# Pairing the first two gate/up tiles by weight instead of by tile, with other warm-up matmuls, a free PSUM unit and other places for the score-value runs

## The chip, the cores and the metric

The kernel runs on one core of one Trainium2 chip. The metric is device time in microseconds. The kernel before took 555.25 us (median of three runs, 555.22 to 555.34). One further execution was profiled: 555.64 us, of which 554.4 us lie between its first and last instruction (the span).

## The reference

The input x has 2048 rows of 576 values. It is normalised row by row, and the result xn goes two ways: through attention with a sliding window of 256 keys, 32 heads of 18 values, and through a gated feed-forward of width 4608. The feed-forward's output gates the attention's. All arrays are bf16.

```python
xn = layernorm(x)
qkv = xn @ wqkv                       # 576 -> 3 * 576
p = softmax(mask(q @ k.T * 18**-0.5)) # 256 keys back, causal
s = (p @ v) @ wo
h = sigmoid(xn @ w_gate) * (xn @ w_up)   # 576 -> 4608, twice
g = silu(h @ w_down)                     # 4608 -> 576
out = x + s * g
```

## The kernel before

The rows are worked in four chunks of 512 (NC, NT). For each chunk the program makes a graph of operations: normalisation (build_ln), value projection (build_v), query/key projections (build_qk), scores and exponentials for eight groups of four heads (build_attn), the score-value products (build_pv), the output projection (build_wo), gate/up and down projections (build_ffn) and the closing element-wise work (build_final). A list scheduler in the kernel's own Python (schedule, L1165) then puts all operations in an order for each engine. It has a cost for every operation and for every hand-over from one engine to another, among them 235 ns for a TensorE step that waits for an earlier TensorE step (TURN_WAIT_NS, L84). Each engine works through its list in order; semaphores carry the dependencies. Loads of weights and inputs are issued by the SP queue, also in its listed order.

TensorE works with its array split into two halves of 64 rows. A pair (L119) is two matmuls, one on each half, that run side by side into two PSUM banks; the contraction of 576 is cut into nine pieces of 64, four blocks of 128 rows (two pieces each) and a remainder of 64. A gate/up tile is 128 of the 4608 columns of w_gate and the same of w_up, for the 512 rows of a chunk. Its step "lo" (half 0) runs four pairs in which one half of the array adds the upper pieces of gate and the other half the lower pieces of up; its step "hi" (half 1) runs the same four pairs with the halves exchanged, and a fifth pair for the remainder. "hi" waits for "lo", since both add into the same two banks.

PSUM is used in four units of two banks. Pool S (units 0 and 1) serves scores, projections and transposes, pool F (units 2, 3, 1) gate/up and down, pool V (all four) the score-value runs (L366 to L368). A unit is taken when the scheduler places an operation, and is free again when the operations that read it are done.

The start is special. Gate and up weights for two tiles come as one load each (load_nat, weights at L960; tiles 0 and 1 share a slot). The 512 rows of the first chunk come in four blocks of 128 that are normalised one by one and transposed on TensorE (L644, recorded as L650); ScalarE and VectorE copy the transposes to xnT (L631). Tiles 0 and 1 (NEARLY = 2) don't wait for all blocks: each is cut into three parts (PARTS, L76), block 0, block 1, and blocks 2 and 3 together, and each part has a lo and a hi step of four pairs without the remainder (early_turn, L128; gate_up, L991). The remainder of the rows is transposed last (build_two, L616) and a single pair per tile adds it (last_rows, L1012). The third tile's lo step is placed ahead of tile 1's last hi step (the name ahead). tail (L1023) is ScalarE's tanh and VectorE's product, after which the tile's unit is free.

Before the first transposes, and again between those of block 0 and block 1, TensorE multiplies a zero tile (warm, L496, sizes in WARM, L72): nine pairs of 512 columns and seven of 128, then five pairs of 256.

The score-value products of four head groups are one run of 256 (first chunk) or 384 TensorE instructions, small matmuls of 19 columns (recorded as L854); there are eight runs. RUN_AT (L43) holds for each the position in TensorE's instruction stream before which it is not placed (L1202).

Of the kernel before, what the change touches and what calls it, by code (L numbers as in the profile page):

```python
# [12 lines left out]
P = 128  # L13
# [5 lines left out]
NT = 512  # L19
NC = S // NT  # L20
BPC = NT // P
FG = 4
NFG = NFT // FG
WG = 2
# [15 lines left out]
OENG = ("SP", "POOL")  # L40
PV_ORDER = (0, -4, 1, 7, 2, -3, 3, 6, 4, -2, -1, 5)
TURN_NS = 265.0
RUN_AT = (2093, 3885, 5836, 7411, 9682, 11471, 13542, 15053)  # L43
BINS = (((-4, 0, 1), (1, 1, 5), (6, 6, 2)),
        ((-2, 0, 3), (3, 3, 5)),
        ((0, 0, 5), (5, 5, 3)),
# [48 lines left out]
def mm_ns(n):  # L95
    return max(24.7, n / 2.4 + 2.7)
# [19 lines left out]
BLOCKS = ((1, 2, 3, 4), (1, 2, 3, 4, 0))  # L116


def pair(eng, outs, lhs, rhs, start, stop, swap=0, parts=False):  # L119
    res = None  # L120
    for i in range(2):
        t = i ^ swap
        res = eng.matmul(outs[i], lhs(ROWS[t], i), rhs(ROWS[t], i), start=start, stop=stop, tile_position=(64 * t, 0),  # L123
                         skip_group_check=parts)
    return res


def early_turn(eng, outs, lhs, rhs, hi, first):  # L128
    res = None
    for k in BLOCKS[0]:  # L130
        res = pair(eng, outs, lambda r, t: lhs(r, t, k), lambda r, t: rhs(r, t, k), first and not hi and k == BLOCKS[0][0], False, hi, True)
    return res
# [13 lines left out]

class Hold:

    __slots__ = ("pool", "n", "units", "rel")

    def __init__(self, pool, n):
        self.pool = pool
        self.n = n
        self.units = None
        self.rel = []

    def release(self, op):
        self.rel.append(op)
# [2 lines left out]
class Pool:  # L161
# [27 lines left out]

    def take(self, hold, units):  # L190
        deps = []
        for u in units:
            if self.last[u] is not None:
                deps += self.last[u].rel
            self.last[u] = hold
        hold.units = units
        return deps


class Op:  # L200
    __slots__ = ("eng", "est", "deps", "fn", "name", "prio", "start", "end", "tok", "needs_tok",
                 "nbytes", "slack", "idx", "succs", "cidx", "odeps", "acq", "lane", "filler", "space", "ni", "run", "then")
# [60 lines left out]
class Builder:  # L263
# [231 lines left out]

    def warm(self, groups, dep, before):  # L496
        h, zero = self.warm_h, self.warm_src
        for n, est, count in groups:
            def f_warm(eng, n=n):
                return pair(eng, self.halves(h, n), lambda r, t: zero[r, :],  # L500
                            lambda r, t: zero[r, :][:, None, :].broadcast_to([64, n // P, P]), True, True)
            for i in range(count):
                w = self.op("PE", est, f_warm, f"warm:{n}:{i}", deps=[dep], prio=4, acq=None if before else h, odeps=[before], ni=4)
                w.filler = h
                h.release(w)
                before = w
# [435 lines left out]
    def build_ffn(self, c):  # L942
        op = self.op
        xs = c % 2
        x_in = self.xnT[:, xs, :, :]
        slots = {}
# [40 lines left out]
        def bank(h, w):  # L987
            o = h.units[0] * 1024 + 512 * w
            return self.ps[:, o:o + 512]

        def gate_up(ft, h, half, acq, part=None, deps=(), behind=()):  # L991
            sw, fc = slots[ft // WG], slice((ft % WG) * P, (ft % WG + 1) * P)
            b0, b1 = (0, BPC) if part is None else PARTS[ft][part]
            t0, n = b0 * P, (b1 - b0) * P
            xin = (self.op_xnT[c] if part is None else self.op_x0)[b0:b1]

            def lhs(r, t, k):
                return self.wgs[r, sw, k - 1, t, fc] if k else self.wgr[r, rslots[ft // (2 * WG)], ft % (2 * WG) * P:(ft % (2 * WG) + 1) * P]

            def f(eng):  # L1000
                outs = [bank(h, w)[:, t0:t0 + n] for w in range(2)]
                if part is None:
                    return turn(eng, outs, lhs, lambda r, t, k: x_in[r, k, t0:t0 + n], half)
                return early_turn(eng, outs, lhs, lambda r, t, k: x_in[r, k, t0:t0 + n], half, part == 0)
            steps = len(BLOCKS[half] if part is None else BLOCKS[0])
            o = op("PE", steps * mm_ns(n), f, f"f1{half}:{c}:{ft}", deps=[xin, wops[ft // WG][0:1 + half if part is None else 1], deps],
                   prio=3 if part is None else 1, odeps=chain[half] if part is None else list(behind), acq=acq, ni=4 * steps)
            chain[half] = [o] if part is None else chain[half] + [o]
            self.ffn_last = o
            return o  # L1010

        def last_rows(ft, h, behind):  # L1012
            fc = slice(ft % (2 * WG) * P, (ft % (2 * WG) + 1) * P)

            def f(eng):
                return pair(eng, [bank(h, w) for w in range(2)], lambda r, t: self.wgr[r, rslots[0], fc], lambda r, t: x_in[r, 0, :],
                            False, True, 1, True)
            o = op("PE", mm_ns(NT), f, f"f12:{c}:{ft}", deps=[self.op_xnT[c], wops[0][1]], prio=1, odeps=behind, ni=4)
            chain[1] = chain[1] + [o]
            self.ffn_last = o  # L1020
            return o

        def tail(ft, h, pg):  # L1023
            st, dt_ = self.r_t.produce()
            th = op("ACT", act_ns(NT), lambda e: e.activation(self.tring[:, st, :], bank(h, 0), ACTF.Tanh, scale=0.5),  # L1025
                    f"th:{c}:{ft}", deps=[pg, dt_], prio=0)
            war = [self.prev_f2_last[ft // FG]] if self.prev_f2_last else []
            mu = op("DVE", dve_ns(NT), lambda e: e.scalar_tensor_tensor(  # L1028
                self.hT[:, ft, :], self.tring[:, st, :], 1.0, bank(h, 1), ALU.add, ALU.mult),
                f"hm:{c}:{ft}", deps=[th, pg, war], prio=0)  # L1030
            h.release(mu)
            self.r_t.release(st, mu)
            hm[ft] = mu
# [3 lines left out]
        if early:  # L1037
            weights(0)
            weights(1)
            hs = [self.pool_f.hold() for _ in range(NEARLY)]  # L1040
            for ft, h in enumerate(hs):
                u = None
                for part in range(len(PARTS[ft])):
                    lo = gate_up(ft, h, 0, None if part else h, part, [u])
                    if ft == early - 1 and part == len(PARTS[ft]) - 1:
                        ahead = self.pool_f.hold()
                        ahead = (ahead, gate_up(early, ahead, 0, ahead))
                        chain[1] = chain[1] + [ahead[1]]
                    u = gate_up(ft, h, 1, None, part, [lo], [ahead[1]] if ahead else [])
                u = last_rows(ft, h, [u] + ([ahead[1]] if ahead else []))  # L1050
                tail(ft, h, u)
                if ft == 1:
                    self.r_w.release(slots[0], u)
        for ft in range(early, NFT):
            if ft % WG == 0 and ft // WG not in slots:
                weights(ft // WG)
            if ahead and ft == early:
                h, lo = ahead
            else:
                h = self.pool_f.hold()  # L1060
                lo = gate_up(ft, h, 0, h)
            u = gate_up(ft, h, 1, None, None, [lo])
# [319 lines left out]
```

## Time and profile before

| | |
|---|---|
| median of three runs | 555.25 us |
| profiled execution | 555.64 us |
| its span | 554.4 us |
| TensorE matmuls | 550.1 us busy, 8234 instructions |
| VectorE | 324.3 us |
| ScalarE | 272.3 us |
| GpSimd | 209.1 us |
| HBM read, written | 63.18 MB, 2.36 MB |

A line of the timeline gives the start in us, the time to the last end of a group in us, engine, source line, operation, output and inputs, the shape and the count; in brackets the idle time of that engine before it and what ended it. A matmul's record is longer than its share of the array, because matmuls overlap; the spacing of starts tells the rate. "PE L123" stands for all pairs, since one helper makes them; what a pair belongs to is read from the tile names (wgs: gate/up weights, wgr: their remainder, wqg: query/key weights, wd_sb: down weights, hT as input of a 512-column matmul: warm-up). The chain of waits is the work that ended last, followed back.

### The profile page before, as it was taken

To read this page: it belongs to the slowest core of one execution; us is meant where nothing else is said; L and a number is where in the kernel's file an instruction comes from. 1 tells how busy PE (TensorE), PEld (TensorE's weight loads), DVE (VectorE), ACT (ScalarE), POOL (GpSimd) and SP (SyncE) were. 2 spreads that over 40 slices of the span, in tenths; PEclk is the share of its full clock that TensorE was granted. 3 is DMA by queue.
4 is the path that set the end of the run, shared out by engine and by line. 5 is a ranking of instruction groups with operands and counts; after the bars stand their busy time and mean duration, and the time that the engine had idled before them with its cause. 6 is when DMAs were issued, how large, how long until landed. Compare 5 with 4: busy or idle time off the path is not lost.

```text
span 554.4 us, 19202 instructions
## 1 busy us (share of the span) xinstructions
PE 550.1 (99%) x8234; PEld 337.2 (61%) x8234; DVE 324.3 (58%) x782; ACT 272.3 (49%) x380; POOL 209.1 (38%) x360
## 2 busy tenths in 40 slices
PE   8999999999999999999999999999999999999998
PEld 5465555767545554577755555557776565445887
DVE  5467564854597654746485655764375564865412
ACT  4246562444265764445355565464446663567202
POOL 5734343564346123085423333164536113270020
DMA  8899999242456657353125765273102656350002
GB/s 231 235 259 246 255 261 271 78 84 53 100 152 173 201 164 201 102 131 69 29 58 162 233 186 154 82 198 86 33 20 66 202 169 178 107 146 3 6 21 67
DMA packets 141212, 75.85 MB, mean 137 GB/s; under 512 B 43676, under 2 KB 139260, under 8 KB 141128
## 3 DMA queue, kind: packets, MB, share of 16 engines
q1 hardware_dynamic: 133704, 68.71, 47.1%
q0 software_dynamic: 7424, 5.92, 4.0%
q8 instruction: 65, 1.06, 0.8%
q14 instruction: 19, 0.16, 0.1%
HBM read 63.18 MB, written 2.36 MB: 118 GB/s over the span
## 4 chain that ended last, share of the span: by engine, by line
PE 98%; DMA 1%; SPq 0%; issue 0%; DVE 0%; ACT 0%
PE ps L123 95%; PE ps L854 3%; DMA wgs<-in_B_w_up_dram 1%; SPq L294 0%; PE ps L650 0%; ACT thf L1139 0%; DVE thf L1141 0%; DVE xf L1144 0%
## 5 line engine op out<-in xcount | busy, mean ns | idle before, releaser
L123 PE MATMUL ps<-xnT,wgs 64*128 64x512 bf16 (+2 forms) x2368 | 283.3, 370 | 0.5 <-DMA wgs<-in_B_w_up_dram 0.5
L804 ACT ACTIVATE expr<-ps 128x1024 bf16<-128x1024 f32 (+4 forms) x160 | 155.0, 969 | 99.3 <-PE ps L123 97.8
L123 PEld LDWEIGHTS ps<-xnT,wgs 64*128 64x128 bf16 x2368 | 114.3, 94 | 110.4 <-ACT xnT L631 0.6
L123 PE MATMUL ps<-wd_sb,hT 64*128 64x288 bf16 (+2 forms) x2448 | 153.8, 276 | 0.0
L1028 DVE SCALAR_TENSOR_TENSOR hT<-tring,ps 128x512 bf16<-128x512 bf16 x144 | 98.7, 685 | 82.9 <-ACT tring L1025 80.5
L1025 ACT ACTIVATE tring<-ps 128x512 bf16<-128x512 f32 x144 | 86.2, 598 | 118.5 <-PE ps L123 115.8
L294 POOL DMA_DIRECT2D qk<-qd x160 | 82.9, 524 | 154.4 <-PE ps L123 150.1
L123 PEld LDWEIGHTS ps<-wd_sb,hT 64*128 64x128 bf16 x2448 | 112.7, 94 | 29.9 <-issue 0.6
L817 DVE TENSOR_TENSOR expr<-expr,mask 128x128 bf16<-128x128 bf16 (+2 forms) x240 | 64.2, 294 | 66.9 <-ACT expr L804 64.5
L294 POOL DMA_DIRECT2D oT<-o2T x72 | 36.6, 516 | 125.6 <-DVE ot L885 70.4
L768 POOL TENSOR_SCALAR kx<-kprev,small 128x256 bf16<-128x256 bf16 x64 | 60.8, 960 | 8.0 <-PE ps L123 7.1
L123 PE MATMUL ps<-qk,kx 64*128 64x320 bf16 (+1 forms) x704 | 59.2, 254 | 0.0
L123 PE MATMUL ps<-xnT,wgr 64*128 64x512 bf16 x288 | 55.0, 376 | 0.0
L123 PEld LDWEIGHTS ps<-qk,kx 64*128 64x128 bf16 x704 | 31.8, 94 | 24.9 <-issue 0.4
L123 PE MATMUL ps<-xnT,wqg 64*128 64x512 bf16 (+1 forms) x320 | 37.8, 355 | 0.0
L689 DVE CAST qd<-ps 128x1024 bf16<-128x1024 f32 (+1 forms) x20 | 22.3, 1116 | 8.9 <-PE ps L123 8.8
L882 DVE STREAM_TRANSPOSE ot<-ps 128x512 f32<-128x512 f32 x32 | 20.2, 685 | 11.8 <-PE ps L854 11.8
L768 DVE TENSOR_SCALAR kx<-qk,small 128x512 bf16<-128x512 bf16 x64 | 21.5, 365 | 7.1 <-PE ps L123 6.3
L123 PEld LDWEIGHTS ps<-xnT,wgr 64*128 64x128 bf16 x288 | 14.4, 94 | 16.6
L890 DVE STREAM_TRANSPOSE o2T<-o 128x512 bf16<-128x512 bf16 x32 | 22.6, 706 | 2.5 <-DMA oT<-o2T 2.2
L123 PEld LDWEIGHTS ps<-xnT,wqg 64*128 64x128 bf16 x320 | 15.3, 94 | 11.4
L936 ACT ACTIVATE s_attn<-ps 128x576 bf16<-128x576 f32 x16 | 10.3, 651 | 22.9 <-PE ps L123 22.9
(71 smaller groups left out, 284.4 us busy)
## 6 DMA issues: line engine op xcount, KB each, us to landing
wgs<-in_B_w_gate_dram SPq DMA_DIRECT2D x72, 256.0 KB, 4.1
wgs<-in_B_w_up_dram SPq DMA_DIRECT2D x72, 256.0 KB, 4.3
wd_sb<-in_B_w_down_dram SPq DMA_DIRECT2D x9, 576.0 KB, 6.5
wqg<-in_A_wqkv_dram SPq DMA_DIRECT2D x32, 128.0 KB, 3.9
qk<-qd POOLq DMA_DIRECT2D x100, 36.0 KB, 2.6
wgr<-in_B_w_gate_dram SPq DMA_DIRECT2D x36, 64.0 KB, 2.9
wgr<-in_B_w_up_dram SPq DMA_DIRECT2D x36, 64.0 KB, 3.2
wvo<-in_A_wqkv_dram SPq DMA_DIRECT2D x4, 576.0 KB, 5.5
```

The costliest lines, as they stand in the source:

```text
L123: res = eng.matmul(outs[i], lhs(ROWS[t], i), rhs(ROWS[t], i), start=start, stop=stop, tile_position=(64 * t, 0), skip_group_check=parts)
L294: o = self.op(eng, DMA_ISSUE_NS[eng], lambda e: e.dma_start(dst, src), name, deps, prio, nbytes=nbytes)
L689: return eng.tensor_copy(dst, self.both(h, n))
L768: return e.tensor_scalar(self.kx[:, sx, pos:pos + n_ // SW, t, :], src.rearrange("p (s k) -> p s k", k=SW), self.half[:, t:t + 1], None, A ...
L804: return eng.activation(self.expr[:, se, :, lo * SW:NT], self.both(h, NT)[:, :, lo * SW:NT], ACTF.Exp, scale=SM_SCALE)
L817: return eng.tensor_tensor(e_, e_, m_, ALU.mult)
L854: res = eng.matmul(outs[i][p0:p0 + VH, cols], self.v_aug[ROWS[i], o:o + VH], self.expr[ROWS[i], se, t, cols], start=m == 0, stop=m == len( ...
L882: return e.transpose(self.ot1[:, p1, :], self.halves(hp, NT, un)[i])
L890: t2 = op("DVE", dve_ns(NT), lambda e, p2=p2, p3=p3: e.transpose(self.o2T[:, p3, :], self.o2[:, p2, :]), f"ot2:{c}:{pr}:{i}", deps=[on, d3 ...
L936: return eng.activation(dst, self.both(h2, 288), ACTF.Copy, scale=1.0 if c == NC - 1 else 0.25)
L1025: th = op("ACT", act_ns(NT), lambda e: e.activation(self.tring[:, st, :], bank(h, 0), ACTF.Tanh, scale=0.5), f"th:{c}:{ft}", deps=[pg, dt_ ...
L1028: mu = op("DVE", dve_ns(NT), lambda e: e.scalar_tensor_tensor(self.hT[:, ft, :], self.tring[:, st, :], 1.0, bank(h, 1), ALU.add, ALU.mult) ...
```

## The change

The first two gate/up tiles are worked together. A pair now holds the same weight of both tiles: gate of tile 0 beside gate of tile 1, then up beside up, for one block of rows at a time (four parts in place of three). So a step needs the load of one weight only, and one block. There are 4 parts x 2 weights x 2 halves = 16 steps of four pairs, where there were 2 tiles x 3 parts x 2 halves = 12, four of them of 256 columns. The pool hands out both units at once (first, Hold.each). The third tile's lo step is placed behind all of them, and the remainder pairs of the two tiles, which keep the old pairing of gate with up, wait for the hi step of the other weight.

The fourth tile takes its PSUM unit from pool V, so that it may have unit 0. Of the warm-ups, the wide ones in front become ten single matmuls over all 128 rows, the narrow ones three pairs, and those behind the first transposes two pairs of 512 columns. RUN_AT has eight new values.

```diff
-RUN_AT = (2093, 3885, 5836, 7411, 9682, 11471, 13542, 15053)
+RUN_AT = (2096, 3832, 5614, 7366, 9427, 10958, 13261, 14786)
-WARM = (((512, 427, 9), (128, 107, 7)), ((256, 160, 5),))
+WARM = (((512, 427, 10, 1), (128, 107, 3, 2)), ((512, 320, 2, 2),))
-PARTS = (((0, 1), (1, 2), (2, 4)),) * NEARLY
+PARTS = ((0, 1), (1, 2), (2, 3), (3, 4))
...
     def take(self, hold, units):
         deps = []
-        for u in units:
+        for j, u in enumerate(units):
             if self.last[u] is not None:
                 deps += self.last[u].rel
             self.last[u] = hold
+            if hold.each:
+                self.last[u] = hold.each[j]
+                hold.each[j].units = [u]
...
-        for n, est, count in groups:
+        for n, est, count, tiles in groups:
+                if tiles == 2:
+                    return pair(...)
+                return eng.matmul(outs[0], zero, zero[:, None, :].broadcast_to([P, n // P, P]), start=True, stop=True)
...
+        def early_pairs(part, w, half, deps, acq=None):
+            b0, b1 = PARTS[part]
+            cols = slice(b0 * P, b1 * P)
+
+            def f(eng):
+                res = None
+                for k in BLOCKS[0]:
+                    res = pair(eng, [bank(h, w)[:, cols] for h in hs], lambda r, t: self.wgs[r, slots[0], k - 1, w, t * P:t * P + P],
+                               lambda r, t: x_in[r, k, cols], part == 0 and not half and k == BLOCKS[0][0], False, half, True)
+                return res
+            o = op("PE", len(BLOCKS[0]) * mm_ns((b1 - b0) * P), f, f"f1{half}:{c}:{'gu'[w]}{part}",
+                   deps=[self.op_x0[b0:b1], wops[0][0][w], deps], prio=1, acq=acq, ni=4 * len(BLOCKS[0]))
...
-        def last_rows(ft, h, behind):
+        def last_rows(ft, h, deps, behind):
-            o = op("PE", mm_ns(NT), f, f"f12:{c}:{ft}", deps=[self.op_xnT[c], wops[0][1]], prio=1, odeps=behind, ni=4)
+            o = op("PE", mm_ns(NT), f, f"f12:{c}:{ft}", deps=[self.op_xnT[c], wops[0][1], deps], prio=1, odeps=behind, ni=4)
...
             hs = [self.pool_f.hold() for _ in range(NEARLY)]
-            for ft, h in enumerate(hs):
-                ...
+            first = self.pool_f.hold(NEARLY)
+            first.each = hs
+            hi = [None, None]
+            for part in range(len(PARTS)):
+                ws = (0, 1) if part < len(PARTS) - 1 else (1, 0)
+                lo = [None, None]
+                for w in ws:
+                    lo[w] = early_pairs(part, w, 0, hi[w], first if part == 0 and w == 0 else None)
+                for w in ws:
+                    hi[w] = early_pairs(part, w, 1, lo[w])
+            ahead = self.pool_f.hold()
+            ahead = (ahead, gate_up(early, ahead, 0, ahead))
+            chain[1] = chain[1] + [ahead[1]]
+            tail(0, hs[0], last_rows(0, hs[0], [hi[1]], [hi[0]]))
+            u = last_rows(1, hs[1], [hi[0]], [hi[1], ahead[1]])
+            tail(1, hs[1], u)
...
-                h = self.pool_f.hold()
+                h = (self.pool_v if ahead and ft == early + 1 else self.pool_f).hold()
```

More of the change, by code (lines that the diff above doesn't have):

```diff
@@ L125, in pair @@
     return res
[L128 to L132, printed above, removed]
 def turn(eng, outs, lhs, rhs, hi):
@@ L147 @@
 class Hold:
-    __slots__ = ("pool", "n", "units", "rel")
+    __slots__ = ("pool", "n", "units", "rel", "each")
     def __init__(self, pool, n):
@@ L155, in __init__ @@
         self.rel = []
+        self.each = None
     def release(self, op):
@@ L497, in warm, with f_warm @@
         h, zero = self.warm_h, self.warm_src
-        for n, est, count in groups:
-            def f_warm(eng, n=n):
-                return pair(eng, self.halves(h, n), lambda r, t: zero[r, :],
-                            lambda r, t: zero[r, :][:, None, :].broadcast_to([64, n // P, P]), True, True)
+        for n, est, count, tiles in groups:
+            def f_warm(eng, n=n, tiles=tiles):
+                outs = self.halves(h, n)
+                if tiles == 2:
+                    return pair(eng, outs, lambda r, t: zero[r, :],
+                                lambda r, t: zero[r, :][:, None, :].broadcast_to([64, n // P, P]), True, True)
+                return eng.matmul(outs[0], zero, zero[:, None, :].broadcast_to([P, n // P, P]), start=True, stop=True)
             for i in range(count):
-                w = self.op("PE", est, f_warm, f"warm:{n}:{i}", deps=[dep], prio=4, acq=None if before else h, odeps=[before], ni=4)
+                w = self.op("PE", est, f_warm, f"warm:{n}:{i}", deps=[dep], prio=4, acq=None if before else h, odeps=[before], ni=2 * tiles)
                 w.filler = h
@@ L989, in bank, with gate_up @@
             return self.ps[:, o:o + 512]
-        def gate_up(ft, h, half, acq, part=None, deps=(), behind=()):
+        def early_pairs(part, w, half, deps, acq=None):
[9 more added lines that the diff above has]
+                   deps=[self.op_x0[b0:b1], wops[0][0][w], deps], prio=1, acq=acq, ni=4 * len(BLOCKS[0]))
+            chain[half] = chain[half] + [o]
+            self.ffn_last = o
+            return o
+        def gate_up(ft, h, half, acq, deps=()):
             sw, fc = slots[ft // WG], slice((ft % WG) * P, (ft % WG + 1) * P)
-            b0, b1 = (0, BPC) if part is None else PARTS[ft][part]
-            t0, n = b0 * P, (b1 - b0) * P
-            xin = (self.op_xnT[c] if part is None else self.op_x0)[b0:b1]
+            n = NT
+            xin = self.op_xnT[c]
             def lhs(r, t, k):
@@ L1000, in f @@
             def f(eng):
[L1001 to L1008, printed above, removed]
+                return turn(eng, [bank(h, w) for w in range(2)], lhs, lambda r, t, k: x_in[r, k, :], half)
+            o = op("PE", len(BLOCKS[half]) * mm_ns(n), f, f"f1{half}:{c}:{ft}", deps=[xin, wops[ft // WG][0:1 + half], deps],
+                   prio=3, odeps=chain[half], acq=acq, ni=4 * len(BLOCKS[half]))
+            chain[half] = [o]
             self.ffn_last = o
             return o
-        def last_rows(ft, h, behind):
+        def last_rows(ft, h, deps, behind):
             fc = slice(ft % (2 * WG) * P, (ft % (2 * WG) + 1) * P)
@@ L1039, in build_ffn @@
             weights(1)
+            assert NEARLY == 2
             hs = [self.pool_f.hold() for _ in range(NEARLY)]
-            for ft, h in enumerate(hs):
[L1042 to L1053, printed above, removed]
+            first = self.pool_f.hold(NEARLY)
[14 more added lines that the diff above has]
+            tail(1, hs[1], u)
+            self.r_w.release(slots[0], u)
         for ft in range(early, NFT):
@@ L1059, in build_ffn @@
             else:
-                h = self.pool_f.hold()
+                h = (self.pool_v if ahead and ft == early + 1 else self.pool_f).hold()
                 lo = gate_up(ft, h, 0, h)
-            u = gate_up(ft, h, 1, None, None, [lo])
+            u = gate_up(ft, h, 1, None, [lo])
             tail(ft, h, u)
```

## The prediction

> **What bounds the kernel now.** I read the page's head and its chain of waits first, to see which engine carries the span; then TensorE's timeline from 5.8 to 16.7 us, where three of the four edits lie; then ScalarE's timeline for the same stretch, to see when the input blocks come; then the neighbourhood of the score-value runs (L854), which the fourth edit moves.
>
> The page:
>
> ```profile
> span 554.4 us, 19202 instructions
> PE 550.1 (99%) x8234; PEld 337.2 (61%) x8234; DVE 324.3 (58%) x782; ACT 272.3 (49%) x380; POOL 209.1 (38%) x360
> ...
> PE 98%; DMA 1%; SPq 0%; issue 0%; DVE 0%; ACT 0%
> ```
>
> TensorE is the bound from its first real matmul to its last. No engine off it can give anything back; only work that TensorE stops doing, or a time when it stands still, counts. So I looked for the standstills. The first is at the start (TensorE's timeline):
>
> ```profile
> 6.08 0.98 PE L123 MATMUL ps<-hT 64*128 64x256 bf16 x10
> 6.93 0.29 PE L650 MATMUL ps<-ident,xnr 64*128 64x64 bf16 x8
> 7.70 0.86 PE L123 MATMUL ps<-xnT,wgs 64*128 64x128 bf16 x24 [0.47 <-DMA wgs<-in_B_w_up_dram]
> 8.39 0.28 PE L650 MATMUL ps<-ident,xnr 64*128 64x64 bf16 x8
> 8.51 0.61 PE L123 MATMUL ps<-xnT,wgs 64*128 64x128 bf16 x16
> 8.96 0.28 PE L650 MATMUL ps<-ident,xnr 64*128 64x64 bf16 x8
> 9.07 1.38 PE L123 MATMUL ps<-xnT,wgs 64*128 64x128 bf16 x32
> 10.27 0.30 PE L650 MATMUL ps<-ident,xn 64*128 64x64 bf16 x8
> 10.39 1.05 PE L123 MATMUL ps<-xnT,wgs 64*128 64x256 bf16 x16
> 11.26 0.40 PE L123 MATMUL ps<-xnT,wgr 64*128 64x512 bf16 x2
> ```
>
> The first gate/up step waits 0.47 us for the up weights (landed 7.56); after it TensorE has work without a break. The gate half of the same slot is complete at 6.01 us by the updates of its semaphore. ScalarE's timeline gives the blocks:
>
> ```profile
> 6.47 0.58 ACT L631 ACTIVATE xnT<-ps 128x512 bf16<-128x512 bf16 x1
> 7.27 0.60 ACT L631 ACTIVATE xnT<-ps 128x512 bf16<-128x512 bf16 x1 [0.22 <-PE ps L650]
> 8.72 0.60 ACT L631 ACTIVATE xnT<-ps 128x512 bf16<-128x512 bf16 x1 [0.85 <-PE ps L650]
> ```
>
> Block 0 is there at 7.05, block 1 at 7.87, block 2 at 9.32, block 3 (VectorE) at 9.70. The other two standstills are near the L854 runs: TensorE's timeline around the third and the sixth run, and the chain's piece inside the sixth.
>
> ```profile
> 225.93 2.41 PE L854 MATMUL ps<-expr,v_aug 64*19 64x320 bf16 x192
> ...
> 229.79 0.55 PEld L123 LDWEIGHTS ps<-xnT,wgs 64*128 64x128 bf16 x8 [0.54 <-ACT expr L804]
> ...
> 400.98 2.84 PE L854 MATMUL ps<-expr,v_aug 64*19 64x320 bf16 x192
> ...
> 402.58 0.14 issue
> ```
>
> The third run takes 2.41 us, the sixth, the same work, 2.84: 0.42 more, with a hole at 402.58 that waits for nothing but issue. At 229.79 a step waits for a PSUM unit that an exponential (L804) still reads: its predecessor began at 229.37 and is 0.21 us longer than the 0.216 of such a pair. That is all: 0.47 at the start, 0.21, 0.42. Everywhere else pair follows pair.
>
> **The change part by part.** *Pairing gate with gate.* The first step now needs block 0 and the gate half alone, so it can begin at 7.05 + 0.06 (the 229.79 step began 0.06 after its exponential ended), say 7.12, behind the transposes of block 1, which stay at 6.93. A step on one block is 8 matmuls, four pairs; 16 of them take 8.51 to 8.96, so one step is 0.22. TensorE works in order, and the second step (up, block 0) needs the up weights and stands ahead of the second half of gate, because that half has to wait 0.235 (the code's own figure) for the first. So one step, and one only, is done before 7.70: -0.22. The queue of loads keeps its order, so the up half still lands at 7.56.
>
> From 7.70 on both versions run the same blocks, and each block's transposes come at the same places (8.39, 8.96, 10.2). Block 2 can be used alone at 9.38, where before blocks 2 and 3 were one part: between the pair at 9.71 and the part at 9.84 TensorE lost 0.08 to block 3, and that goes: -0.08. Cutting that part in two turns 16 pairs of 256 columns (109 ns each, eight of them 10.39 to 11.26) into 32 of 128 (56 ns): +0.04. Steps of 0.22 follow each other in two chains, where each has to be 0.235 behind its own predecessor; the trace shows 0.24 from 7.92 to 8.16 for such a step. Some eight more such handovers cost between 0 (transposes between them) and 0.02 each; I take +0.05. Before, the equivalent end of the early work was 11.26 + 0.435 (the last part of tile 1, done at 12.35 behind the third tile's first half) = 11.70; now 11.70 - 0.21 = 11.49. The row pairs on the remainder (L1012) need the last transposed piece, ready at 11.20: no wait. They now wait for the early steps of the other bank, and the third tile's first half (0.86 us), which stands between, hides that; without it each would wait 0.235.
>
> *The fourth tile's unit.* Both first tiles now end together: 11.49, then the third tile's first half (0.86), then two remainder pairs, 12.57 and 12.79. Before, a unit came back 1.54 after its remainder pair (11.48 to 13.02, ScalarE 0.60 and VectorE 0.69 in it), so now near 14.1, and the second's near 14.8. The fourth tile is due at 13.87 and would in the old rotation begin 0.3 late; in unit 0, whose last reader ended at 11.20, it begins on time. The fifth is due at 14.7, its unit free at 14.1. Cost 0; unit 0 is next asked for by the first projection at 19.69.
>
> *Warm-ups.* Nine pairs at 0.427 and seven at 0.107 become ten single 512-column matmuls and three pairs: 4.59 before, 4.59 after. They end before the first transposes in both cases (idle 5.61 to 5.88). Behind those, 5 x 256 columns (6.08 to 6.93) become 2 x 512, at most 0.85, and block 0 is not there before 7.05. Cost 0, with cover until 7.12. The granted clock reads 1.000 throughout, but the pairs' spacing shows a slow clock at first: 0.197 per 256-column pair at 6.49, 0.110 at 6.69; so it opens at about 6.6.
>
> *Runs re-placed.* L854's work is unchanged (2.35 us a run, eight runs). The floors move up to 513 instructions earlier; the values they need were complete 2 to 14 us ahead, 0.5 for the fourth, whose place its data set (it began 237 instructions behind its floor). Their output moves on the SP and POOL queues go with them; weights queued behind them on SP landed at least 1.4 us ahead of their first use after 20 us (issues matched with landings), against some 0.5 an issue. What can change is the 0.42 and the 0.21. The instruction queue moved 65 blocks of 16 KB for TensorE's 16,732 instructions, 257 a block; the last block transfer before the sixth run's stall ended 0.28 us after that run's start, those of the other five long runs 0.3 to 2 us before theirs, and these five lost nothing. The floors of the six, taken modulo 256, were 204, 243, 210, 207, 230, 205 and are 238, 198, 211, 206, 205, 194: four of six lie earlier in their block, so that the transfer starts later. Gain bound: both gone, -0.63. Loss bound: two more runs hit, +0.84. The nearest row, one run of six hit, says about as many as before, so 0 for the 0.42; of the 0.21, one such wait behind eight runs, I take a fifth as gone, -0.04.
>
> The Trainium skill, "Runtime: NRT & Kernel Launch", Instruction fetch mechanics, says that blocks of 256 instructions are fetched ahead and that a crossing is mostly hidden. The trace agrees on the size and not on the hiding in one run of eight; by the page the re-placing would be worth 0 and the sum -0.21 instead of -0.25.
>
> **Sum.** -0.22 - 0.08 + 0.04 + 0.05 - 0.04 = -0.25. The profiled execution took 555.64 (span 554.4 and 1.24 around it), which gives 555.39; the median of the runs is 0.39 lower, 555.25, and gives **555.0**. That gap is close to the 0.42 stall, which may be in the profiled execution alone.
>
> **The rivals.** *A: the standstills at the runs go too.* For it: seven of eight runs lost nothing, so none need to. Against: the earlier places in the block. 555.0 less 0.2 to 0.6: 554.4 to 554.8. *B: the change does nothing.* If the second step is not what waits but the chain of blocks sets the pace, the early work ends at 11.7 again: 555.2 to 555.3. Against it: only 0.08 was lost to blocks. *C: more runs starve.* Each costs 0.42, as the sixth did; from one more on the kernel is slower than before: 555.4, with two or three 555.8 to 556.3. *D: the clock opens late*, since other matmuls now keep TensorE busy before it, and its cover is thinner by 0.58 us (7.70 less 7.12). Every microsecond past 7.1 at the cold clock (107 ns a pair against 56) loses half a microsecond; past about 9.8 us it decides, 1.35 lost against 0.25 gained. If it takes the 5.6 us that it took before (1.05 to 6.6) once more from 7.1, 2.8 are lost: 556.4 to 557.8. Against it: singles over 128 rows and pairs over 64 + 64 occupy the array as long and as fully.
>
> The Trainium skill, "TensorE: Matmul & The Clock Gate", Part 1, has the clock rise after a busy window of about 3.4 us that runs free of the kernel's start. The trace fits one full window before 6.6; by that rule a window missed costs half of 3.4, 1.7 us, which is D's lower part.
>
> **How the numbers follow.** The forecast (554.9 to 555.2) 0.42, A 0.16, B 0.11, C 0.14, D 0.07, and 0.10 for an order of work that I don't foresee, half on either side. What a measurement of this kernel tells from no change is taken as 0.2%, 1.11 us: 554.14 to 556.36. Forecast, A, B and C lie inside: 0.83 less 0.01 for C's end. Slower: D, half of the unforeseen, C's end: 0.13. Faster: the other half, 0.05, since all standstills together (1.10) just reach it. The range leaves out A's end, C's end, D and the unforeseen: 554.5 to 556.1.
>
> **What would show it.** First gate/up matmul near 7.12 (x8), the next at 7.70; transposes at 8.39; remainder pairs done near 12.8; no wait before the fourth tile; 512-column pairs at 0.216 after 7; the eight L854 groups at 2.4 us each. Wrong it would be if pairs after 7.1 stand 0.107 apart, if L854 groups take 2.8, or if the first step still begins at 7.7.

## The result, and the profile after

The changed kernel takes 558.59 us (median of six runs, 558.00 to 561.28) against 555.35 for the kernel before in the same comparison: ratio 1.0063, 95% interval 1.0042 to 1.0085. That is 3.2 us slower, above the predicted range (554.5 to 556.1). The profiled execution took 559.73, with a span of 558.4 against 554.4.

The head of the page and its chain say that TensorE still carries the span, and does no more work than before; loads (DMA) take 2% of the chain in place of 1%:

```profile
span 558.4 us, 19223 instructions
PE 549.5 (98%) x8244; PEld 338.0 (61%) x8244; DVE 324.6 (58%) x782; ACT 270.7 (48%) x380; POOL 208.8 (37%) x360
...
PE 97%; DMA 2%; ACT 0%; issue 0%; SPq 0%; DVE 0%; POOL 0%
```

So the 4.0 us are standstills. TensorE's timeline at the start:

```profile
5.89 0.29 PE L650 MATMUL ps<-ident,xnr 64*128 64x64 bf16 x8 [0.92 <-DVE xnr L563]
7.20 0.29 PE L650 MATMUL ps<-ident,xnr 64*128 64x64 bf16 x8 [0.59 <-DVE xnr L563]
7.58 1.08 PE L123 MATMUL ps<-xnT,wgs 64*128 64x128 bf16 x32
...
12.55 0.59 PE L123 MATMUL ps<-xnT,wgr 64*128 64x512 bf16 x4
12.98 1.03 PE L123 MATMUL ps<-xnT,wgs 64*128 64x512 bf16 x8
```

The four steps on block 0 (x32) run without a break. The two remainder pairs take from 12.55 to 12.98. The prediction's sum has them done at 12.79, so 0.2 earlier; in the kernel before the second of them ended at 13.00. In this execution the start is neither gain nor loss. The first large hole is at 57 to 62 us (same view):

```profile
57.63 0.30 PE L123 MATMUL ps<-qk,kx 64*128 64x320 bf16 x2
58.26 1.90 PE L123 MATMUL ps<-xnT,wgs 64*128 64x512 bf16 x16 [0.32 <-DMA wgs<-in_B_w_up_dram]
59.98 0.40 PE L123 MATMUL ps<-xnT,wgr 64*128 64x512 bf16 x2
60.20 0.29 PE L123 MATMUL ps<-qk,kx 64*128 64x256 bf16 x2
62.32 1.04 PE L123 MATMUL ps<-xnT,wgs 64*128 64x512 bf16 x8 [1.84 <-DMA wgr<-in_B_w_gate_dram]
```

Tile 20's lo step waits for its up weights, its hi step for the remainder weights. Before, the same two-matmul steps stood there, and the next one followed 0.11 to 0.13 later:

```profile
57.66 0.31 PE L123 MATMUL ps<-qk,kx 64*128 64x320 bf16 x2
57.79 1.03 PE L123 MATMUL ps<-xnT,wgs 64*128 64x512 bf16 x8
...
59.73 0.28 PE L123 MATMUL ps<-qk,kx 64*128 64x256 bf16 x2
59.84 1.03 PE L123 MATMUL ps<-xnT,wgs 64*128 64x512 bf16 x8
```

Start to start, the first wait costs 0.63 - 0.13 = 0.50 and the second 2.12 - 0.11 = 2.01. SP's queue after the change shows what the two loads stand behind (start, time of the issue):

```profile
51.04 2.43 SPq L296 DMA_TRANSPOSE xnT<-xnr  x1
53.52 0.57 SPq L291 DMA_DIRECT2D wgs<-in_B_w_gate_dram  x1
54.13 0.50 SPq L291 DMA_DIRECT2D wgs<-in_B_w_up_dram  x1
54.68 0.51 SPq L291 DMA_DIRECT2D wd_sb<-in_B_w_down_dram  x1
55.23 1.55 SPq L296 DMA_TRANSPOSE xnT<-xnr  x1
56.83 0.60 SPq L291 DMA_DIRECT2D wgr<-in_B_w_gate_dram  x1
57.47 0.59 SPq L291 DMA_DIRECT2D wgr<-in_B_w_up_dram  x1
```

The remainder weights were issued at 56.83 and 57.47 and landed at 61.95 and 62.23. Before, they were issued at 52.87 and 53.70, had landed by 59.42 and were used at 61.57.

The second hole is in the fifth score-value run (TensorE's timeline):

```profile
334.91 1.62 PE L854 MATMUL ps<-expr,v_aug 64*19 64x320 bf16 x115
338.16 1.11 PE L854 MATMUL ps<-expr,v_aug 64*19 64x320 bf16 x77 [1.62 <-issue]
339.20 1.04 PE L123 MATMUL ps<-xnT,wgs 64*128 64x512 bf16 x8
```

The run takes 339.20 - 334.91 = 4.29 in place of 2.35, and the hole waits for nothing but issue: 1.94 lost. The 0.42 of the sixth run before is gone. 0.50 + 2.01 + 1.94 - 0.42 = 4.0, the difference of the spans.

### The profile page after: what moved, and what is told of

It reads as the page before. It is cut to its first block, busy times and chain, and to the rows that moved or that the text cites. A ratio compares the mean times of both kernels' runs of the same rounds, so it can differ in the third digit from the quotient of the medians.

```text
span 558.4 us, 19223 instructions
## 1 busy us (share of the span) xinstructions
PE 549.5 (98%) x8244; PEld 338.0 (61%) x8244; DVE 324.6 (58%) x782; ACT 270.7 (48%) x380; POOL 208.8 (37%) x360
## 4 chain that ended last, share of the span: by engine, by line
PE 97%; DMA 2%; ACT 0%; issue 0%; SPq 0%; DVE 0%; POOL 0%
PE ps L123 94%; PE ps L854 3%; DMA wgr<-in_B_w_gate_dram 1%; DMA x<-in_A_x_dram 1%; ACT tring L639 0%; SPq L291 0%; ACT tring L637 0%; ACT xnT L631 0%; PE ps L650 0%; ACT thf L1155 0%; DVE thf L1157 0%; POOL small L638 0%; DVE xf L1160 0%
## 5 line engine op out<-in xcount | busy, mean ns | idle before, releaser
L123 PE MATMUL ps<-xnT,wgs 64*128 64x512 bf16 (+1 forms) x2400 | 283.7, 368 | 2.2 <-DMA wgr<-in_B_w_gate_dram 1.8
L751 DVE CAST v_aug<-ps 64x288 bf16<-64x288 f32 x32 | 14.5, 453 | 10.6 <-PE ps L123 10.0
```

The source lines that it names most:

```text
L751: return eng.tensor_copy(dst, src)
```

## The experiments

In what follows "place" is a run's position in TensorE's instruction stream, as the kernel's own scheduler counts it. The trace records each block of instructions as it is fetched, 256 instructions in 16 KB. A block's fetch mostly begins about when TensorE passes the edge that opens the block before it; "its edge" below is that one, and a fetch is early or late against it.

Four of the kernels below, those of the first, second, fourth and eighth experiment, don't compute the reference's result (relative error 0.198). early_pairs looks up the units of the first two tiles under the name hs, and it does so only when the program is written out. By then build_ffn has bound hs again, to the units of the chunk's last two down projections. In the changed kernel these are units 2 and 3 in the same order, so its result is right by luck. In the four kernels the planner has them as 3 and 2, and each of the two tiles adds its early steps into the other's unit. The order of the work, its shapes and its semaphores are the planner's all the same, so their times are read here as those of the same work with two PSUM addresses exchanged; that the exchange itself costs no time was not tried. None of the four is a kernel to use.

### Each part put back

First: the changed kernel with the fourth tile's unit as before.

```diff
-                h = (self.pool_v if ahead and ft == early + 1 else self.pool_f).hold()
+                h = self.pool_f.hold()
```

> The changed kernel, but the fourth tile takes its unit from pool F as before. Theory 1 (the fourth tile's free unit pulls tile 20 two microseconds forward and puts other loads ahead of its remainder weights, so TensorE waits 2.4 us near 60 us): that wait goes, 555.5 to 556.5. Theory 2 (the re-placed runs starve for instructions, 1.9 us at the fifth): nothing changes in that, 558 to 559. Theory 3 (the paired start and its warm-ups cost the time): 558 to 559.

Measured 556.88, ratio 1.003 (1.0016 to 1.0043). Tile 20's hi step is at 61.27, its remainder weights landed at 58.88, and no wait is there. The fifth run starves as after the change:

```profile
332.36 1.64 PE L854 MATMUL ps<-expr,v_aug 64*19 64x320 bf16 x115
335.71 1.11 PE L854 MATMUL ps<-expr,v_aug 64*19 64x320 bf16 x77 [1.71 <-issue]
```

The twelve runs fall into two groups, five at 555.24 to 555.81 and seven at 556.5 to 559.4, which is what a hole of some 2 us present in some executions would give; only the profiled one (557.24) shows it directly. So two separate losses: the late weights go with the free unit, the hole does not.

Second: the changed kernel with the old floors.

```diff
-RUN_AT = (2096, 3832, 5614, 7366, 9427, 10958, 13261, 14786)
+RUN_AT = (2093, 3885, 5836, 7411, 9682, 11471, 13542, 15053)
```

> The changed kernel with the eight old floors of RUN_AT. Theory 1: the wait near 60 us stays at about 2.4 us, 556.5 to 558. Theory 2: the 1.9 us at the fifth run goes, 555 to 556.5 and no L854 group above 2.9 us. Theory 3: 558 to 559.

Measured 558.57, ratio 1.0065 (1.0051 to 1.0079). The fifth run is whole, but two others starve (timeline around the third and the fourth run):

```profile
224.09 1.62 PE L854 MATMUL ps<-expr,v_aug 64*19 64x320 bf16 x122
226.32 0.98 PE L854 MATMUL ps<-expr,v_aug 64*19 64x64 bf16 x70 [0.61 <-issue]
...
276.83 2.40 PE L854 MATMUL ps<-expr,v_aug 64*19 64x320 bf16 x190
280.65 0.25 PE L854 MATMUL ps<-expr,v_aug 64*19 64x192 bf16 x2 [1.42 <-issue]
```

The other executions (558.07 to 560.88) lost more than this one (557.76), and no trace shows where. The pairing changes the number of instructions ahead, so the old floors put the runs elsewhere. These holes show where TensorE stops. The third run began at instruction 5837 and stopped after 122 matmuls (244 instructions): 6081. The fourth stopped at 7749 + 380 = 8129, the fifth run of the changed kernel at 9435 + 230 = 9665. Modulo 256 all three are 193: TensorE stops at the edge between two blocks. The runs had begun 13, 133 and 27 instructions behind an edge.

Third: the changed kernel, with the first 104 loads of SP in the order that they had before.

```diff
...
+        of = {}
+        for o in prog["SP"][:len(SP_ORDER)]:
+            of.setdefault(o.name, []).append(o)
+        prog["SP"][:len(SP_ORDER)] = [of[n].pop(0) for n in SP_ORDER]
         self.prog = prog
```

> The changed kernel, TensorE's order untouched, but the first 104 loads on the SP queue are issued in the order that they had in the kernel before. Theory 1: if the order of the loads is the cause, the remainder weights of tile 20 land near 59.5 and the wait falls from 2.4 us to under 0.5: 555.5 to 556.5. If tile 20 being early is the cause, the wait falls by less than half: 557 to 558.5. Theory 2 and 3: 558 to 559.

Measured 557.20, ratio 1.0038 (1.0024 to 1.0053). The remainder weights landed at 59.83 and were used at 59.92, and TensorE had stood still for 0.35 us for them. So the old order of loads doesn't give the old margin: TensorE's order is what changed. The planner has tile 20's hi step at 59.37 (before: 61.23) and tile 22's lo step at 61.53 (before: 64.88). The fifth run starved, 2.06 us.

This execution (559.21) lost something else behind that hole: the granted clock is 0.51 from 337.0 to 340.4 us, and 1.00 behind it. The 512-column step at 337.23 takes 1.69 us in place of 0.86. 3.4 us at half the clock are 1.7 lost. Four of the twelve executions (558.85 to 559.21) have the same mean clock, 0.997, and so has one of the six of the change (561.28). A hole as long, 2.04 in the fifth experiment's profile, left the clock at 1.00, so when this happens is not shown.

Fourth: the pairing alone, with the old floors, warm-ups and unit.

> The pairing of the first two tiles alone: old warm-ups, old floors, fourth tile in pool F. Theories 1 and 2: neither stall, first gate/up matmul near 7.1 to 7.6, 554.8 to 555.8. Theory 3: the start is slower, 557 to 559.

Measured 557.62, ratio 1.0042 (1.003 to 1.0054). The planner's own end is 0.93 later here (552.58 against 551.65), and the matmuls behind the fourth run starve, 32 matmuls and 2.1 us after its end, again at an edge (7680 + 448 = 8128, 192 modulo 256):

```profile
273.55 2.41 PE L854 MATMUL ps<-expr,v_aug 64*19 64x320 bf16 x192
275.89 2.13 PE L123 MATMUL ps<-wd_sb,hT 64*128 64x288 bf16 x32
278.46 0.67 PE L123 MATMUL ps<-wd_sb,hT 64*128 64x288 bf16 x8 [0.43 <-issue]
```

The profile's own loss is 1.4 in span; the rest of the 2.3 was not followed. These four say where the losses are, and that the runs move with the parts.

### The two causes taken away

Fifth: four loads ahead on SP's queue. Sixth: six loads moved behind the fifth run. Seventh: both.

```diff
+        sp = prog["SP"]
+        j = next(i for i, o in enumerate(sp) if o.name == "flip:x:4")
+        first = [o for o in sp if o.name in ("dma:w:0:10", "dma:wgr:0:10")]
+        sp[:] = [o for o in sp[:j] if o not in first] + first + [o for o in sp[j:] if o not in first]
...
+        late = next(o for o in prog["PE"] if o.name == "f11:2:18")
+        for o in prog["SP"]:
+            if o.name.startswith(("dma:w:2:12", "dma:wq:3:1:", "dma:wqr:3:1:")):
+                o.deps = o.deps + [late]
```

> The changed kernel, with four loads placed earlier on SP's queue: the gate/up weights of tiles 20 and 21 and the remainder weights of tiles 20 to 23 are issued ahead of the transposing load of the next input block (issue 2.4 us), the down-weight load and a second transposing load. All else as changed. Theory 1 (the remainder weights come too late at 60 us because they are queued behind those slow issues: 0.5 + 2.0 us lost): the wait at 57.6 to 62.3 us goes, and the time is 558.6 - 2.4 = 556.2. Rival (the transfers are late whatever their place in the queue, because the memory system is full there): the wait stays, 558.0 to 558.6. The fifth score-value run still starves in both.

Measured 558.09, ratio 1.0056 (1.0037 to 1.0075): 0.5 less than the change, not 2.4, and the two intervals overlap for the most part. The waits at tile 20 are gone, the first of the remainder weights landing at 56.59. So the profiled execution after the change had met an unusually late queue: in the second and the sixth experiment, with the same order of loads, the remainder weights landed 0.09 and 0.18 us ahead of their use. The margin that was over 2 us is near zero, and the traced executions lose between nothing and 2.5.

> The changed kernel, with six loads moved away from the fifth score-value run: the weights w of slot 12 and the query/key weights of the next chunk, issued at 332.6 to 335.9 us, additionally wait for a gate/up step behind the run (they are first used 13 us or more later). The run keeps its place in the instruction stream. Theory 2 (the block of instructions that the run needs is fetched late because its transfer stands behind those loads): the fetch begins about 1.5 us ahead of the run as at the other runs, the 1.9 us hole goes, 558.6 - 1.9 = 556.7. Rival (the place is at fault: the run begins only 27 instructions behind an edge between two blocks, so the time is too short): hole and 558.6 stay.

Measured 557.39, ratio 1.0035 (1.0024 to 1.0047): 1.2 less than the change. The chain of waits at the fifth run:

```profile
332.97 1.41 PE ps L854 x108
334.38 0.94 issue
335.32 1.11 PE ps L854 x44
```

The run's block was fetched from 0.10 us after the run's start (0.94 after the change), and the hole shrank from 1.62 to 0.94. These loads are at most part of the cause: the DMA engines were 0.26 busy from 331 to 333, and the fetch still began 1.8 us after TensorE had passed its edge (near 331), where those of the runs at the same place (the sixth to the eighth, 27 or 28 behind) began 0.3 to 1.0 ahead of it. Just before that edge, though, other loads kept the engines busy (1.12 from 329 to 330, 0.51 in the next microsecond).

> The changed kernel with both load edits: the weights at 57 us earlier, the six loads at 333 us later. If theories 1 and 2 hold, what is left of the change is its gain at the start: 558.6 - 2.4 - 1.9 = 554.3, faster than before by 1.0 at most. If only theory 1 holds 556.2, if only theory 2 holds 556.7. If the new pairing, units or warm-ups themselves cost time, it stays above 555.4 with both waits gone from the profile.

Measured 557.09, ratio 1.0033 (1.0021 to 1.0045), far from 554.3. Its profile has a hole at the fifth run that costs some 1.4 us, a wait of 0.25 us at tile 22, and a first up step 1.2 behind the planner's, since the up weights landed at 8.56 in this execution.

Eighth: the kernel of the first experiment, its fifth floor raised from 9427 to 9467.

> The kernel of the first experiment (changed, but the fourth tile's unit from pool F: 556.9) with the fifth floor raised by 40: its run then begins 40 instructions further behind the block's edge (66 in place of 26), all other runs where they were; the planner's own end is 0.23 us later. The block is then asked for about 2 us earlier in relation to the run. Theory 2 and its rival both expect the hole to go or shrink below 0.5: 556.9 - 1.9 + 0.2 = 555.2, or less by up to 0.3 where the profile's 2.2 us excess is the usual size. If the hole is not due to instructions, but to the run's values or units, 556.9 to 557.1 stays.

Measured 555.96, ratio 1.0014 (1.0005 to 1.0024), and ten of twelve executions within 0.4 us. The run begins 66 instructions behind the edge and is whole but for 0.1:

```profile
334.85 2.53 PE L854 MATMUL ps<-expr,v_aug 64*19 64x320 bf16 x192
337.31 0.40 PE L123 MATMUL ps<-qk,kx 64*128 64x64 bf16 x6
```

One number takes the hole out of the profile and 0.9 off the median, with 0.23 more in the planner's own end. Two of the twelve executions lie above 556.5, seven of the first experiment's. The two intervals overlap, though, and five executions of the first were faster than all but one of these, so it is the long executions that go. The edit also changed more than the run's distance from its edge: with the six loads issued at the same distance from that edge, the block's fetch began 0.3 late here and 2.4 late in the first experiment.

Ninth: the changed kernel with five floors raised, so that the six long runs begin 37 to 59 behind an edge.

```diff
-RUN_AT = (2096, 3832, 5614, 7366, 9427, 10958, 13261, 14786)
+RUN_AT = (2096, 3832, 5614, 7382, 9444, 10990, 13284, 14836)
```

> The changed kernel with five of the eight floors raised by 16 to 50, so that the six long score-value runs begin 37 to 59 instructions behind the edge between two instruction blocks, where the change has them at 21 to 47. The planner's own end rises by 0.1 us (551.5 to 551.6). Loads as in the change. Theory 2 (the place of the fifth run lets the instructions come too late): the 1.9 us hole goes, 558.6 - 1.9 = 556.7, and what is left above the kernel before is the late remainder weights (0 to 2.4 us an execution). Rival (the hole follows the loads at 333 us, wherever the run lies): 557.5 to 558.6.

Measured 556.32, ratio 1.0021 (1.0013 to 1.003): 2.2 less than the change. All six runs take 2.4, and one wait is left in the profile:

```profile
59.12 0.27 PE L123 MATMUL ps<-qk,kx 64*128 64x256 bf16 x2
59.90 1.04 PE L123 MATMUL ps<-xnT,wgs 64*128 64x512 bf16 x8 [0.50 <-DMA wgr<-in_B_w_gate_dram]
```

Tenth: these floors with both load edits.

> The same floors with both load edits of the seventh experiment (weights of tiles 20 to 23 ahead at 50 us, six loads behind the run at 333 us). If these two causes are all of the loss, this is the kernel before less what the planner gives (551.6 against 551.65) and what the start gives (0 to 0.3): 554.9 to 555.2. If the pairing, the free unit or the warm-ups cost time of their own, it stays above 555.6 without a hole or a wait in its profile.

Measured 556.76, ratio 1.003 (1.0018 to 1.0041): no better than the ninth, so a cause was missing. Tile 20 no longer waits. Tile 22 does, for the up weights one place further back in the queue:

```profile
61.46 0.38 PE L123 MATMUL ps<-qk,kx 64*128 64x320 bf16 x4
62.56 1.04 PE L123 MATMUL ps<-xnT,wgs 64*128 64x512 bf16 x8 [0.72 <-DMA wgs<-in_B_w_up_dram]
```

### Parts in the kernel before

Eleventh: the kernel before with the eight new floors.

> The kernel before with the eight new floors alone. Its runs begin 143, 69, 62, 15, 25, 21, 25 and 4 instructions behind an edge. The planner's own end is 0.54 us later (552.19 against 551.65): 555.7 if no run starves. Theory 2: the fifth run, at the same place and beside the same loads as in the change, loses about 2 us, and the eighth, 4 behind its edge, about 1: 557.5 to 558.7. The prediction's view (places cost nothing but the planner's difference): 555.7.

Measured 556.37, ratio 1.0021 (1.0011 to 1.0031): 1.1 slower, of which the planner's end explains 0.54. The chain has small holes at the fourth and the eighth run, 15 and 4 behind their edges, and none at the fifth:

```profile
265.59 1.52 PE ps L854 x107
267.12 0.14 issue
267.26 0.98 PE ps L854 x71
...
334.14 2.34 PE ps L854 x176
...
511.45 1.56 PE ps L854 x114
513.02 0.32 issue
513.34 0.97 PE ps L854 x66
```

Here theory 2 was wrong about the fifth run. At 25 behind an edge, the DMA engines 0.88 busy from 331 to 333, its block was fetched 1.7 us ahead of the run. The place says how much time there is; it doesn't say when the fetch begins.

Twelfth: the kernel before with the free unit alone (the line of the first experiment the other way round).

> The kernel before with the fourth tile's unit from pool V alone. Runs stay where they were to one instruction; the planner's own end is 0.38 us later (552.03). If the free unit by itself makes the remainder weights late, a wait shows at tile 20 and the time is 556 to 558; if that needs the pairing with it (the planner has tile 20 at 61.4 us here, as before, and at 59.4 in the change), only the planner's difference shows: 555.5.

Measured 555.57, ratio 1.0011 (1.0002 to 1.002): the planner's difference and no wait. The free unit makes weights late only with the pairing.

### The whole loss taken back

Thirteenth: the floors of the ninth, and the weights of tiles 20 to 23 all ahead.

```diff
...
+        first = [o for o in sp if o.name in ("dma:w:0:10", "dma:wgr:0:10", "dma:w:0:11")]
...
```

> The floors of the ninth experiment, and six loads ahead on SP's queue at 50 us: the gate/up weights of tiles 20, 21 and of 22, 23, and the remainder weights between them, all ahead of the transposing load (2.4 us), the down weights and the second transposing load. In the tenth experiment, with only the first four ahead, tile 20 no longer waited, but tile 22 did (0.72 us), for the weights one place further back. Theory 1 in its new form (the change places tile 20 two and tile 22 three us earlier than before, in a stretch where the DMA engines have no time to spare, so a wait only moves to the next load in the queue): with these two tiles served first no wait is left at 57 to 63 us and 556.3 becomes 555.2 to 555.6; if the next loads in the queue become late in their turn, a wait of 0.5 to 1 us shows at another place before 75 us and 556.0 to 556.7 stays. Rival (the rest of the loss is in the pairing itself): 556.3 without such a wait.

Measured 555.71, ratio 1.0004 (0.9994 to 1.0013): level with the kernel before. Tiles 20 and 22 follow without a wait:

```profile
59.48 0.27 PE L123 MATMUL ps<-qk,kx 64*128 64x256 bf16 x2
59.59 1.03 PE L123 MATMUL ps<-xnT,wgs 64*128 64x512 bf16 x8
...
61.53 0.38 PE L123 MATMUL ps<-qk,kx 64*128 64x320 bf16 x4
61.75 1.03 PE L123 MATMUL ps<-xnT,wgs 64*128 64x512 bf16 x8
```

Above the kernel before of its own comparison, the change stood 3.2 us, with other floors 1.1 (the ninth), with the six loads ahead besides 0.25. So the floors are worth about 2.2, the order of the loads about 0.8, and what is left is not told from nothing. The pairing, the free unit and the warm-ups show no cost of their own here, and no gain either. In the traces the first query/key projection (wqg), which has the same work ahead of it in both, begins at 19.08 to 20.47 us in the nine with the whole changed start (median 19.44) and at 19.39 to 19.99 in the four with the old one (median 19.77): 0.3 earlier, inside the scatter.

Fourteenth: the kernel before, with floors that put its long runs 43 to 64 behind an edge.

```diff
-RUN_AT = (2093, 3885, 5836, 7411, 9682, 11471, 13542, 15053)
+RUN_AT = (2093, 3599, 5604, 7676, 9700, 11508, 13556, 15084)
```

> The kernel before with other floors: the six long runs begin 43 to 64 instructions behind a block edge (before: 22 to 44), the planner's own end 0.27 us earlier (551.38 against 551.65). Theory 2: no run starves in the profile, the time is 555.25 - 0.3 = 555.0, and the spread of the executions is no wider than before (1.4 us). Rival (places behind an edge don't matter, other things decide): a hole of 0.4 or more at some run, 555.2 or later.

Measured 556.22, ratio 1.0015 (1.0007 to 1.0024): a miss. No run starved inside, but at the fourth run, 64 behind, the matmuls after it lost 0.3, as in the fourth experiment. There the run ends 64 instructions short of a second edge, where one that begins 27 behind its edge ends 101 short of it. The seventh run began 64 behind as well and lost nothing, so the distance alone doesn't decide. Most of its loss is elsewhere, in the chain's end:

```profile
545.12 0.47 DVE xf L1144
545.60 3.20 DMA out_dram<-xf
548.82 3.90 DMA xf<-in_A_x_dram
```

The last reload of x waits for an output to leave its buffer; the planner's end is TensorE's, and doesn't see it. So this run decides nothing about the edges, and no version here beats both kernels.

## Why the prediction was wrong

**The start: right in its mechanism, worth less than its noise.** The first step was to begin at 7.12 and to be done before 7.70. It began at 7.58 in the profile after the change, since ScalarE's copy of block 0 ended only at 7.53, and at 7.02 to 7.31 in the first four experiments. But the up weights, issued at about 3.14 each time, landed anywhere from 6.79 to 8.56 in the fifteen profiles that record it; "the up half still lands at 7.56" took one execution for the rule. A term of 0.22 can't be seen beside 1.8 of scatter. The rest of the start kept the order that was forecast and came 0.2 late: remainder pairs done at 12.98 (forecast 12.79), the fourth tile at 14.06 (13.87) without a wait. The clock had opened before the first gate/up step (16 pairs of 128 columns from 7.58 to 8.50), so rival D did not come about. The warm-ups were not tried alone.

**"Cost 0" for the fourth tile's unit was the first step that failed.** It asked only who waits for units 0 to 3. It didn't ask what the scheduler does with the rest of the first chunk once the fourth tile begins 0.3 earlier: with the pairing it puts the tiles behind it forward, tile 20's hi step by 1.9 and tile 22's lo step by 3.3 against the kernel before. (With the fourth tile's unit as before, in the first experiment, both are within 0.2 of where they were.) In that stretch the DMA engines had no time to spare already before: their share from 55 to 60 us was 1.23 (it can pass 1, as packets overlap), so a step put forward finds weights that can't come sooner. "Weights landed at least 1.4 us ahead of first use" was measured in the order before and used for another order. Worth about 0.8 in the medians, 2.5 in the profiled execution.

**"0 for the 0.42" of the re-placed runs was the second, and the larger.** Rival C named the mechanism (other runs starve) with a chance of 0.14, but at 0.42 each. One run starved, for 1.94: the term was under-sized more than fourfold, and with it the loss bound of 0.84. Even rival C's three runs, 556.3, lie 2.3 under the result. The prediction also compared floors modulo 256, not places. By places the six long runs stand 22 to 44 behind their edges before and 21 to 47 after, nearly the same, so nothing in them foretold the hole. What differs is when the block is fetched. Over all sixteen traces, leaving the first blocks out, a fetch began 0.2 us ahead of its edge (median of 678) where the DMA engines were under 0.7 busy in the 2 us ahead of it, with 13% over 1 us late; above that it began 0.8 behind its edge (median of 266), with 39% over 1 us late. That is a count of what goes together; no experiment shows the busy engines to be the reason.

The Trainium skill, "Runtime: NRT & Kernel Launch", Instruction fetch mechanics, has such a crossing mostly hidden. These traces agree for the most part and put a price on the rest: 0.3 to 2.1 us a hole, each counted one at an edge.

**What stays open.** Why the fetch for the fifth run still began 1.8 us late with the six loads moved away (sixth and seventh experiment), and 0.3 late at the same edge in the eighth. Other loads before the edge (1.12 busy in the sixth, 1.08 in the seventh) may have a part in it, but in the eleventh the engines were as busy (1.07 from 331 to 332) and the fetch was on time.

## What to carry to other kernels

A change at one end of a listed program re-times everything behind it: ask of the new order, not of the old, which loads have lost their lead, above all where the DMA engines are full. Very short instructions in long runs eat a block of instructions faster than the next one arrives (384 in 2.35 us here, so 256 in 1.6, where a fetch and what follows it took 2.1 to 2.9); count where the runs stand between block edges before and after, and price a miss by the longest hole seen, not by the first. When a fix only moves a wait to the next load in the queue, the load order needs mending as a group.

## What the runs showed of the hardware

- Behind 7.2 us, TensorE stood still with nothing to wait for, over 0.3 us from one start to the next, fourteen times in the sixteen traces. By the traces' own count of its instructions each was at 193 modulo 256. The longest was 2.06 us of idle time (third experiment).
- A fetch of 16 KB mostly took 0.9 to 1.4 us, and the work behind the edge went on 1.2 to 1.5 us after its end (2.00 after the run's start at the fetch's end, 3.25 at the first matmul, after the change).
- One and the same load, issued at 3.14 us, landed between 6.79 and 8.56 us.
- A transposing load mostly held SP's queue for 1.2 to 2.4 us, others mostly for 0.5 to 0.7.
- Behind a hole of 2.06 us the granted clock was 0.51 for 3.4 us (third experiment); behind one of 2.04 (fifth) it stayed at 1.00.
